# Layer norm, dilated local attention and a gated MLP on one core: half the turns of x move from TensorE to DMA and VectorE, attention's exponentials and loads move back in ScalarE's order

## The chip, the core and the metric

The kernel runs on one core of a Trainium2 chip. The core has five engines with queues of their own: TensorE (matmuls; PE, and PEld for its weight loads), VectorE (DVE), ScalarE (ACT), GpSimd (POOL) and SyncE (SP), and 16 DMA engines. SP and ACT can issue transfers. TensorE writes its results to PSUM; the other data lies in SBUF, 128 partitions wide. The metric is the device time of one execution in microseconds; lower is better.

## The reference

S is 2048, D is 512, F is 1792. There are 32 heads of 16 values; each position looks at 8 keys, 2 apart, ending with itself.

```python
xn = _layernorm(A_x)
q, k, v = split(xn @ wqkv)                        # 32 heads of 16
idx = pos[:, None] - arange(8)[None, :] * 2       # negative: masked
logits = where(mask, einsum("bhsd,bhswd->bhsw", q, kg) * 0.25, -1e9)
o = einsum("bhsw,bhswd->bhsd", softmax(logits), vg)
s = o @ wo
h = relu(xn @ w1 + b1) ** 2
g = silu(h @ w2 + b2)
out = x + s * g
```

All inputs and the output are float32.

## The kernel before

**Products.** Every large product is made in three passes of float32r: each operand is split into a high part (a float32r copy, by ScalarE) and a low part (what is left, by VectorE or GpSimd), and `PASSES` multiplies high by high, high by low and low by high. A group is 12 matmuls of 128 x 128 by 128 x 512 (four parts of the contraction by three passes) into one PSUM tile. PSUM has three sets of buffers: `acc` (four, `psA`), `h` (two, `psH`) and `tp` (two, `psT`).

**First stage: q, k and v.** x is worked in 16 tiles of 128 rows, in pairs. For tile t, `mean` and `spread` (ScalarE, small work on GpSimd) give the moments, `norm` writes `xn`, `trans` turns it by four TensorE transposes into a `tp` tile, ScalarE copies the high part to `xt`, and `lowx` makes the low part on VectorE. `qkv(t, s)` is a group for s = 0, 1, 2 (q, k, v); ScalarE evacuates it to `stg`, and behind the second tile of a pair the pair goes to the scratch tensors `sq`, `sk` and `sv` in DRAM. The loop (line 508) takes two tiles a, a + 1 a pass, six groups, while the next pair is turned and the pair after that is normalised. The high and low parts of x of tiles 4 to 15 go to the scratch tensor `sx` for the MLP.

**Attention** runs on VectorE (products and sums, no matmul) in 8 units of 256 rows. For a unit: q and k are loaded from DRAM, four steps `qk` (a multiplication and a reduction each), `soft_a` (maximum, subtraction, and the exponential on ScalarE), `soft_b` (sum, reciprocal, multiplication), four steps `av` (again a multiplication and a reduction), `store`. The steps `av` of unit u − 1 stand behind `soft_a` of unit u. q, k and v have one buffer each.

**Second stage: MLP and output.** Four chunks of 512 rows. `up(c, f)` for f = 0 to 13 is a group into one of the two `h` buffers; ScalarE applies relu and the square and writes the high part; `lowh(f)` on VectorE reads the same `h` buffer and makes the low part; `down` for f − 2 adds 12 matmuls to four `acc` tiles. `load_o(u)` loads unit u of attention: it stands in step 7 (u = 2c) and step 12 (u = 2c + 1). `trans_o` turns it by VectorE's 32 x 32 transposes (the load has already moved whole blocks to their places), `lowo` makes the low part, `out_product` multiplies by wo, `gate` adds b2 and applies silu, `finish` multiplies, adds x and stores. The output tiles of the second unit of a chunk are finished in the next chunk, those of the last chunk at the end.

**Who sets the order.** TensorE, VectorE, ScalarE and GpSimd keep the order of the program (`Ordered`, line 62, records each instruction). Two clocks are summed while the program is written: `clock["PE"]` by 227 ns for a matmul and 150 for a transpose, `clock["V"]` by elements per partition / 0.96 + 170 ns for an instruction (lines 41 and 51). Attention is a generator: it yields the due time of its next piece, and `pump` (line 300) lets pieces into VectorE's order while `clock["V"]` plus that time is at most `clock["PE"]` plus a margin (3000 ns in the first stage, −500 or 1000 in the second). `not_before` moves VectorE's clock forward where it has to wait. If a unit isn't stored when `load_o` asks for it, the loop there pumps until it is:

```python
while done_units[0] <= u:
    pump(clock["V"] - clock["PE"] + 4000)
```

The transfers on SP have no such order; the framework's scheduler places them.

Of the kernel before, what the change touches and what calls it, by code (L numbers as in the profile page):

```python
# [14 lines left out]
P = 128  # L15
# [23 lines left out]
WARM2 = 3  # L39

MATMUL, TRANSPOSE, DVE_FIXED, SLACK, LATE, ROOM = 227, 150, 170, 500, 3000, 1000


@with_exitstack
def body(ctx: ExitStack, tc: tile.TileContext, x, wqkv, wo, w1, b1, w2, b2, out):
# [121 lines left out]
    mask = const.tile([P, BI, W], F32, name="mask")  # L167
    zero = px.tile([HALO, 4, P], F32, name="zero")

    def constants():  # L170
        G.memset(zero, 0.0)
# [10 lines left out]
    b2t = const.tile([P, D], F32, name="b2t")  # L182

# [7 lines left out]

    done_tiles = dict(qk=0, v=0)
    done_units = [0]

    def load_u(what, u):
        n = BI if what == "q" else WIN
        src = dict(q=sq, k=sk, v=sv)[what]

        t = att.tile([P, n, P], F32, name=f"{what}{u}", tag="k" if (what, u) == ("v", NU - 1) else what)
        row = src[0, u * UP:u * UP + 1, :]  # L200
        ap = bass.AP(tensor=row.tensor, offset=row.offset, ap=[[BI * P, NB], [src.shape[1] * P, 4], [1, n * P]])
        dma(t.rearrange("p i c -> p (i c)"), ap)
        return t

    def attention():

        tiles, Ls, sums = {}, {}, {}
# [13 lines left out]

        def soft_a(u):
            yield 1500
            L = Ls[u]
            if u == 0:
                lm = L.rearrange("p (i h) w -> p i h w", h=8)
                V.tensor_add(lm, lm, mask[:, :, None, :].to_broadcast([P, BI, 8, W]))
            mx = att.tile([P, BI * 8], F32, name=f"mx{u}", tag="mx")  # L230
            V.tensor_reduce(out=mx, in_=L, axis=AX.X, op=OP.max)
            V.tensor_sub(L, L, mx[:, :, None].to_broadcast([P, BI * 8, W]))
            A.activation(L, L, AF.Exp)

        def soft_b(u):
            yield 2100
            L = Ls[u]
            sm = att.tile([P, BI * 8], F32, name=f"sm{u}", tag="sm")
            V.tensor_reduce(out=sm, in_=L, axis=AX.X, op=OP.add)
            V.reciprocal(sm, sm)  # L240
            V.tensor_mul(L, L, sm[:, :, None].to_broadcast([P, BI * 8, W]))

        def av(u, s):
            i0 = 2 * s
            v, L = tiles["v", u], Ls[u]
            yield 2400
# [18 lines left out]
        def load(u, names):  # L265
            if u < NU:
                while done_tiles[names] < 2 * (u + 1):
                    yield None
                for n in names:
                    tiles[n, u] = load_u(n, u)  # L270

        yield from load(0, "qk")
        not_before(clock["PE"] + 8000)
        yield from load(0, "v")

        for u in range(NU + 1):
            if u < NU:
                Ls[u] = att.tile([P, BI * 8, W], F32, name=f"L{u}", tag="L", bufs=2)
                for s in range(4):
                    yield from qk(u, s)  # L280
                yield from soft_a(u)
                yield from load(u + 1, "qk")
                if u == NU - 1:
                    yield from load(u, "v")
            if u == 0:
                yield from soft_b(0)
            for s in range(4):
                if u > 1 or (u == 0 and s < 2) or (u == 1 and s >= 2):
                    yield from av(max(u - 1, 0), s)
            if u:  # L290
# [38 lines left out]
    NT = S // P  # L329
    mv, means, rs, shifts, xn, pTs, xt, xT, seen = {}, {}, {}, {}, {}, {}, {}, {}, {}  # L330

# [25 lines left out]
    def norm(t):  # L357
        xn[t] = px.tile([P, D], F32, name=f"xn{t}", tag="xn", bufs=2)
        if t < 2:
            n = D // 2 if t == 0 else D  # L360
            for i in range(0, D, n):
                V.tensor_scalar(xn[t][:, i:i + n], xins[t][:, i:i + n], mv[t][:, 0:1], rs[t],
                                op0=OP.subtract, op1=OP.mult)
            del xins[t]
        else:
            A.activation(xn[t], xins.pop(t), AF.Identity, bias=shifts.pop(t), scale=rs[t])
        if t + 4 < NT:
            load_x(t + 4)

    def place(t):  # L370
        if t < TPC:
            xt[t] = xT[0][:, t]
        else:
            xt[t] = pxT.tile([P, 2, KT, P], FR, name=f"xt{t}", tag="xt", bufs=4)

    def trans(t):
        place(t)
        pTs[t] = psT(f"pxT{t}")
        for kt in range(KT):
            PE.transpose(pTs[t][:, kt * P:(kt + 1) * P], xn[t][:, kt * P:(kt + 1) * P], ident)  # L380
        seen[t] = clock["PE"] + 800
        A.activation(xt[t][:, 0], pTs[t].rearrange("p (k n) -> p k n", k=KT), AF.Copy)
# [7 lines left out]
    def qkv(t, s, between=None):  # L390
        if t % 2 == 0:
            stgs[s] = pstg.tile([P, 4, 2, P], F32, name=f"stg{t}_{s}", tag="stg", bufs=4)
        ps = psA(f"pq{t}_{s}")
        n = 0
        for kt in range(KT):
# [3 lines left out]
            if between and kt == 1:  # L399
                between()  # L400
        A.activation(stgs[s][:, :, t % 2], ps.rearrange("p (g c) -> p g c", g=4), AF.Copy,
                     scale=0.25 if s == 0 else 1.0)
        if t % 2:
            r0 = (t - 1) * P + (0 if s == 0 else HALO)
            dst = (sq, sk, sv)[s][:, r0:r0 + UP, :].rearrange("g (p e) c -> p g (e c)", e=2)
            dma(dst, stgs[s].rearrange("p g e c -> p g (e c)"))
            done_tiles["qk" if s < 2 else "v"] = t + (s > 0)

# [27 lines left out]


    sts = [px.tile([P, 6], F32, name=f"st{t}", tag="st", bufs=2) for t in range(2)]
    V.bn_stats(sts[0], xins[0])
    moments(0, sts[0])  # L440
    high(*wq_parts(0, 0))
    norm(0)
    low(*wq_parts(0, 0), G)
    V.bn_stats(sts[1], xins[1])
    moments(1, sts[1])
    xT[0] = xTa.tile([P, TPC, 2, KT, P], FR, name="xT0", tag="xT")
    place(0)
    pT = [psT(f"pxT0_{kt}") for kt in (0, 2)]
    for kt in range(KT):
        PE.transpose(pT[kt // 2][:, kt * P:(kt + 1) * P], xn[0][:, kt * P:(kt + 1) * P], ident)  # L450
    for n in range(WARM2):
        PE.transpose(warm[:, :P], ident, ident)
    for kt in (0, 2):
        hi, lo = (xt[0][:, h, kt:kt + 2] for h in range(2))
        src = pT[kt // 2][:, kt * P:(kt + 2) * P].rearrange("p (k n) -> p k n", k=2)
        A.activation(hi, src, AF.Copy)
        V.tensor_sub(lo, src, hi.bitcast(F32))
        if kt == 0:
            high(*wq_parts(0, 1))
    low(*wq_parts(0, 1), V)  # L460
    norm(1)
    split(*wq_parts(0, 2), G)
    split(*wq_parts(0, 3), V)
    clock.update(PE=8000.0, V=10000.0)

    def highs(s, kt):
# [6 lines left out]

    def first():
        trans(1)
        highs(1, 0)
        mean(2)

    qkv(0, 0, first)
    lowx(1)  # L480
    lows(1, 0)
    spread(2)
    qkv(1, 0, lambda: highs(1, 2))
    lows(1, 2)
# [23 lines left out]
    for a in range(2, NT, 2):  # L508
# [11 lines left out]
        qkv(a, 0)  # L520
        if more:
            trans(a + 2)
        pump(LATE)
        qkv(b, 0)
        weights(a - 5)
        if more:
            lowx(a + 2)
            trans(b + 2)
        if later:
            mean(b + 4)  # L530
        pump(LATE)
        qkv(a, 1)
        if later:
            spread(a + 4)
        if more:
            lowx(b + 2)
        pump(LATE)
        if not more:
            up(0, 0)
        qkv(b, 1)  # L540
        if later:
            spread(b + 4)
        if not more:
# [5 lines left out]
        qkv(a, 2)  # L549
        if later:  # L550
            norm(a + 4)
        pump(LATE)
        qkv(b, 2)
        if later:
            norm(b + 4)
        if a == NT - 4:
            dma(b1t, b1.rearrange("(f p) -> p f", p=P))
            dma(b2t, b2[None, :].to_broadcast([P, D]))
        if a >= TPC:
# [69 lines left out]

    wot = p2.tile([P, 2, 4, 512], FR, name="wot")  # L630

    for c in range(NCH):
# [113 lines left out]
```

## Time and profile before

| | us |
|---|---|
| median of 3 runs | 505.66 (503.79 to 506.11) |
| the profiled execution | 507.61 |
| its span | 505.8 |
| matmul on TensorE, busy | 495.2 |
| VectorE, busy | 418.4 |
| ScalarE, busy | 214.2 |
| granted TensorE clock, share of full | 0.998 |

The profile is of one execution. Its rows have the start in us, the duration, the engine, the line, the operation, output <- input, shape and count; in brackets stands the idle time before it and what ended it. Merged rows (x12, x48) cover several instructions. A matmul's duration holds its way through the array, so rows overlap; the distance from start to start is its cost. Most line numbers are that of the recording helper (L74), so rows are told apart by the tiles: `pq` is a group of `qkv`, `pxT` a transpose of x, `ph` is `up`, `pb` is `down`, `pw` is `out_product`, `pr` and `L` are the steps `qk`, `pv` and `v` the steps `av`, `h` on DVE is `lowh`. In this trace, the matmul that is first of the MLP starts at 144.0 us.

### The profile page before, as it was taken

The numbers are of one execution on the slowest core, as the hardware profiler recorded it, in microseconds if no ns is written. First come the engines' busy times: TensorE is split into PE (matmuls) and PEld (weight loads), VectorE is DVE, ScalarE is ACT, GpSimd is POOL, SyncE is SP. The second block draws the span as 40 slices with busy tenths as digits, with TensorE's granted clock in tenths as the row PEclk, the third lists the DMA queues.
The fourth block names the chain that finished last, engine by engine and source line by source line (L and its number), as shares of the span: only waits on it lengthen the run. The fifth ranks groups of instructions, "written<-read, shape, count | busy, mean of one in ns | idle before, by whom it ended". The sixth has DMA issues, their size and how long they took to land.

```text
span 505.8 us, 5934 instructions
## 1 busy us (share of the span) xinstructions
PE 495.2 (98%) x2209; PEld 406.4 (80%) x2209; DVE 418.4 (83%) x327; ACT 214.2 (42%) x393; POOL 119.5 (24%) x127
## 2 busy tenths in 40 slices
PE   7999989999999999999999999999999999999996
PEld 5788878878787888888888888888888878888885
DVE  5208999999999999997799999589998859995244
ACT  4955275573333556431722442263224136223321
POOL 3622076484000399700203000020200002120000
PEclk9999999999999999999999999999999999999999
DMA  8888787689947774643323515344241612112022
GB/s 293 248 260 296 250 322 230 237 312 338 323 141 238 210 227 141 193 165 158 114 65 144 198 41 183 140 123 158 75 173 33 238 44 84 62 64 83 0 84 84
DMA packets 45064, 85.64 MB, mean 169 GB/s; under 512 B 4988, under 2 KB 28908, under 8 KB 42220
## 3 DMA queue, kind: packets, MB, share of 16 engines
q1 hardware_dynamic: 44172, 78.98, 47.2%
q10 hardware_dynamic: 864, 6.29, 3.4%
q8 instruction: 17, 0.28, 0.2%
q14 instruction: 11, 0.09, 0.1%
HBM read 57.94 MB, written 27.32 MB: 169 GB/s over the span
## 4 chain that ended last, share of the span: by engine, by line
PE 70%; DVE 17%; issue 4%; ACT 3%; DMA 3%; POOL 3%; POOLq 0%; ACTq 0%; DVEq 0%
PE pb L74 30%; PE ph L74 29%; PE pw L74 9%; DVE L L74 5%; DVE pr L74 5%; DMA x<-in_A_x 3%; PE pq L74 3%; DVE v L74 2%; DVE pv L74 2%; ACT scratch L74 1%; POOL rs L74 1%; POOL wq L74 1%; DVE xt L74 1%; ACT stg L74 1%; DVE xn L74 1%
## 5 line engine op out<-in xcount | busy, mean ns | idle before, releaser
L74 PE MATMUL pb<-w,h 128*128 128x512 f32 x672 | 160.6, 389 | 0.0
L74 PEld LDWEIGHTS pb<-w,h 128*128 128x128 f32 x672 | 126.1, 188 | 26.2
L74 PE MATMUL ph<-xU,w 128*128 128x512 f32 x504 | 120.7, 390 | 0.0
L74 ACT ACTIVATE ph<-ph,b1t 128x512 f32<-128x512 f32 x56 | 37.0, 661 | 193.0 <-PE ph L74 187.3
L74 PEld LDWEIGHTS ph<-xU,w 128*128 128x128 f32 x504 | 94.3, 188 | 20.6 <-DVE h L74 0.9
L74 PE MATMUL pq<-wq,xt 128*128 128x512 f32 x432 | 101.6, 392 | 0.9 <-ACT stg L74 0.9
L74 PEld LDWEIGHTS pq<-wq,xt 128*128 128x128 f32 x432 | 80.3, 188 | 17.8 <-ACT stg L74 1.4
L74 DVE TENSOR_TENSOR pr<-k,q 128x2048 f32<-128x2048 f32 x32 | 77.0, 2407 | 14.0 <-DMA x<-in_A_x 13.6
L74 DVE TENSOR_TENSOR pv<-v,L 128x2048 f32<-128x2048 f32 x32 | 75.6, 2362 | 0.5
L74 DVE TENSOR_TENSOR h<-ph,h 128x512 fp32r<-128x512 f32 x56 | 38.4, 685 | 42.8 <-ACT ph L74 42.8
L74 DVE TENSOR_REDUCE L<-pr 128x128 f32<-128x2048 f32 x32 | 73.0, 2282 | 0.7
L74 DVE TENSOR_REDUCE v<-pv 128x256 f32<-128x2048 f32 x32 | 72.9, 2280 | 0.6
L74 POOL TENSOR_TENSOR z<-z,xr 128x512 f32<-128x512 f32 x12 | 21.2, 1778 | 219.3 <-DVE z L74 212.5
L74 PE MATMUL pw<-wot,oT 128*128 128x512 f32 (+1 forms) x204 | 45.5, 376 | 0.0
L74 ACT ACTIVATE stg<-pq 128x512 f32<-128x512 f32 x48 | 28.3, 595 | 35.6 <-PE pq L74 35.6
L74 PEld LDWEIGHTS pw<-wot,oT 128*128 128x128 f32 x204 | 36.8, 188 | 7.1
L74 PE MATMUL ph<-xT,w 128*128 128x512 f32 x168 | 40.6, 391 | 0.1
L74 PEld LDWEIGHTS ph<-xT,w 128*128 128x128 f32 x168 | 31.5, 188 | 7.1 <-DVE h L74 0.5
L74 PE MATMUL pq<-wq,xT 128*128 128x512 f32 x144 | 36.2, 402 | 0.6 <-DVE wq L74 0.4
L74 POOL TENSOR_TENSOR w<-w1r,w 128x512 fp32r<-128x512 f32 x14 | 22.1, 1580 | 60.9 <-DMA rwo<-in_A_wo 49.6
L74 POOL TENSOR_TENSOR w<-w2r,w 128x512 fp32r<-128x512 f32 x14 | 34.5, 2466 | 0.0
L74 ACT ACTIVATE h<-ph 128x512 fp32r<-128x512 f32 x56 | 33.7, 601 | 1.8
(54 smaller groups left out, 325.7 us busy)
## 6 DMA issues: line engine op xcount, KB each, us to landing
k<-sk SPq DMA_DIRECT2D x8, 1408.0 KB, 8.2
v<-sv SPq DMA_DIRECT2D x8, 1408.0 KB, 7.9
sx<-xt SPq DMA_DIRECT2D x12, 512.0 KB, 4.8
xU<-sx ACTq DMA_DIRECT2D x6, 1024.0 KB, 5.7
x<-in_A_x SPq DMA_DIRECT2D x16, 256.0 KB, 6.0
sq<-stg SPq DMA_DIRECT2D x8, 512.0 KB, 5.2
q<-sq SPq DMA_DIRECT2D x8, 512.0 KB, 4.2
sk<-stg SPq DMA_DIRECT2D x8, 512.0 KB, 4.9
```

The lines of the kernel that those rows point to most:

```text
L74: return tc.keep_in_program_order(f(*a, **k))
```

## The change

- **x of tiles 6 to 15** (`TURN = 6`). `norm` writes the pair's `xn` in blocks of 32 columns; `shuffle` moves, by 16 transfers from SBUF to SBUF, block a of rows 32b to 32b + 31 to partitions 32a to 32a + 31 of a tile `xb` that shares two buffers with `xn`; `trans` turns 32 x 32 blocks by one VectorE instruction into the same `tp` tile as before. In the loop, `spread`, `norm`, `trans` and `lowx` of these tiles move: `norm` from behind groups 5 and 6 to behind groups 2 and 3, `trans` one group later, `lowx` likewise.
- **Exponentials.** `soft_a` no longer issues the exponential; `defer` keeps it until `clock["PE"]` has passed `clock["V"]` + 5000 ns, and the next `pump` emits it. `soft_b` waits for that. Unit 0's softmax is done in two halves.
- **Loads of q, k and v** are issued by ScalarE's queue instead of SP, and are deferred likewise; their landing is foreseen 9500 ns after they are emitted, and `qk` and `av` are not placed earlier.
- **First q product.** Tile 0's product with the q weights takes four float32 matmuls from unsplit x and weights (`x0`, `raws`); three transposes that filled time (`WARM2`) and the GpSimd part of these splits go.
- **Places.** `zero` shares the buffer of q; `b2t` is loaded at the start of the second stage.

```diff
+TURN = 6
+BEHIND, LAND, LOAD = 5000, 6000, 9500
...
-        dma(t.rearrange("p i c -> p (i c)"), ap)
+        A.dma_start(t.rearrange("p i c -> p (i c)"), ap)
...
+    behind = []
+
+    def defer(t, f):
+        behind.append((t, f))
+        behind.sort(key=lambda b: b[0])
+
+    def flush(t):
+        while behind and (t is None or behind[0][0] <= t):
+            behind.pop(0)[1]()
...
         def qk(u, s):
             i0 = 2 * s
+            yield from there("k", u)
...
+        def there(n, u):
+            while (n, u) not in tiles:
+                yield None
+            not_before(landing[n, u])
...
-            A.activation(L, L, AF.Exp)
+            def exp():
+                A.activation(L, L, AF.Exp)
+                exps.add((u, h))
+
+            defer(clock["V"] + BEHIND, exp)
...
+        def soft_b(u, h=None):
+            while (u, h) not in exps:
+                yield None
...
+            def start():
                 for n in names:
                     tiles[n, u] = load_u(n, u)
+                    landing[n, u] = clock["PE"] + LOAD
+
+            defer(max(clock["V"] + BEHIND if u else 0, done_tiles[names][1][u] + LAND), start)
...
-        not_before(clock["PE"] + 8000)
...
         limit = clock["PE"] + margin
+        flush(clock["PE"])
...
+            A.activation(xn[t // 2 * 2][:, :, t % 2].rearrange("p a (k c) -> p k a c", k=KT),
+                         xins.pop(t).rearrange("p (k a c) -> p k a c", a=4, k=KT),
+                         AF.Identity, bias=shifts.pop(t), scale=rs[t])
...
+    def shuffle(t):
+
+        src = xn.pop(t)
+        xb[t] = px.tile([P, 4, 2, P], F32, name=f"xb{t}", tag="xn", bufs=2)
+        for b in range(4):
+            for a in range(4):
+                dma(xb[t][32 * a:32 * a + 32, b], src[32 * b:32 * b + 32, a])
...
+            V.transpose(out=pTs[t].rearrange("p (k b n) -> p b k n", k=KT, n=32),
+                        in_=xb[t // 2 * 2][:, :, t % 2].rearrange("p b (k c) -> p b k c", k=KT))
+            seen[t] = clock["V"] + 800
...
+    ps = psA("pq0_0")
+    for kt in range(KT):
+        if kt == KT - 1:
+            trans(1)
+        PE.matmul(ps, x0[:, kt * P:(kt + 1) * P], raws[0, kt], start=kt == 0, stop=kt == KT - 1)
     lowx(1)
+    evacuate(0, 0, ps)
+    highs(1, 0)
     lows(1, 0)
+    mean(2)
+    clock.update(PE=12000.0, V=12500.0)
...
     def load_o(u):
         while done_units[0] <= u:
+            flush(None)
             pump(clock["V"] - clock["PE"] + 4000)
```

More of the change, by code (lines that the diff above doesn't have):

```diff
@@ L435, in lowh @@
         V.tensor_sub(h[:, 1], ph, h[:, 0].bitcast(F32))
[L438 to L464, printed above, removed]
     def highs(s, kt):
@@ L472, in lows @@
         low(*wq_parts(s, kt + 1), G)
[L474 to L479, printed above, removed]
+    sts = [px.tile([P, 6], F32, name=f"st{t}", tag="st", bufs=2) for t in range(2)]
+    V.bn_stats(sts[0], xins[0])
+    moments(0, sts[0])
+    high(*wq_parts(0, 0))
+    norm(0)
+    xT[0] = xTa.tile([P, TPC, 2, KT, P], FR, name="xT0", tag="xT")
+    place(0)
+    pT = [psT(f"pxT0_{kt}") for kt in (0, 2)]
+    for kt in range(KT):
+        PE.transpose(pT[kt // 2][:, kt * P:(kt + 1) * P], xn[0][:, kt * P:(kt + 1) * P], ident)
+    V.bn_stats(sts[1], xins[1])
+    moments(1, sts[1])
+    low(*wq_parts(0, 0), V)
+    x0 = scratch(0)
+    for kt in (0, 2):
+        cols = slice(kt * P, (kt + 2) * P)
+        A.activation(x0[:, cols], pT[kt // 2][:, cols], AF.Copy)
+    norm(1)
+    for kt in range(1, KT):
+        split(*wq_parts(0, kt), V)
+    split(xt[0][:, 0], xt[0][:, 1], x0.rearrange("p (k n) -> p k n", k=KT), V)
+    ps = psA("pq0_0")
+    for kt in range(KT):
+        if kt == KT - 1:
+            trans(1)
+        PE.matmul(ps, x0[:, kt * P:(kt + 1) * P], raws[0, kt], start=kt == 0, stop=kt == KT - 1)
     lowx(1)
+    evacuate(0, 0, ps)
+    highs(1, 0)
     lows(1, 0)
+    mean(2)
+    clock.update(PE=12000.0, V=12500.0)
+    qkv(1, 0, lambda: highs(1, 2))
     spread(2)
-    qkv(1, 0, lambda: highs(1, 2))
     lows(1, 2)
@@ L520, in body @@
         qkv(a, 0)
-        if more:
+        if a + 2 < TURN:
             trans(a + 2)
+        if later:
+            spread(a + 4)
+            mean(b + 4)
         pump(LATE)
@@ L525, in body @@
         weights(a - 5)
-        if more:
+        if a + 2 < TURN:
+            lowx(a + 2)
+            trans(b + 2)
+        elif more:
+            trans(a + 2)
+        if later:
+            norm(a + 4)
+            spread(b + 4)
+        pump(LATE)
+        qkv(a, 1)
+        if a + 2 < TURN:
+            lowx(b + 2)
+        elif more:
             lowx(a + 2)
@@ L529, in body @@
         if later:
[L530 to L536, printed above, removed]
+            norm(b + 4)
+            shuffle(a + 4)
         pump(LATE)
@@ L630, in body @@
     wot = p2.tile([P, 2, 4, 512], FR, name="wot")
+    b2t = p2.tile([P, D], F32, name="b2t")
+    dma(b2t, b2[None, :].to_broadcast([P, D]))
     for c in range(NCH):
```

83 lines of the change are left out of this document (49 added, 34 removed).

## The prediction

> **What bounds the kernel now.** I read the page first, then TensorE in order of time, then what the other engines were late with, then VectorE's end against TensorE's steps in the last two chunks.
>
> ```profile
> span 505.8 us, 5934 instructions
> PE 495.2 (98%) x2209; PEld 406.4 (80%) x2209; DVE 418.4 (83%) x327; ACT 214.2 (42%) x393; POOL 119.5 (24%) x127
> DVE  5208999999999999997799999589998859995244
> ```
>
> TensorE is busy for 98% of the span, so time can only come from matmul work taken off it or from its few gaps. VectorE (the slices) is full from about 40 us to the middle of the run and has holes later: it is the engine whose place in order matters.
>
> ```profile
> 46.20 2.91 PE L74 MATMUL pq<-wq,xt 128*128 128x512 f32 x12
> 48.95 0.60 PE L74 MATMUL pxT<-ident,xn 128*128 128x128 f32 x4
> 49.31 3.02 PE L74 MATMUL pq<-wq,xt 128*128 128x512 f32 x12
> ...
> 67.84 0.66 PE L74 MATMUL pxT<-ident,xn 128*128 128x128 f32 x4 [1.45 <-ACT xn L74]
> ...
> 102.75 0.66 PE L74 MATMUL pxT<-ident,xn 128*128 128x128 f32 x4 [0.18 <-ACT xn L74]
> ...
> 132.98 11.18 PE L74 MATMUL pq<-wq,xt 128*128 128x512 f32 x48 [0.95 <-ACT stg L74]
> 144.00 2.94 PE L74 MATMUL ph<-xT,w 128*128 128x512 f32 x12
> ```
>
> The first row is the start of `qkv(4,0)`, the last that of `up(0,0)`: 97.80 us for 33 groups of 12 matmuls. A group is 2.72 us (the rows of the chain below), 33 are 89.76. So **8.0 us** of this stage are no group: the transposes of tiles 6 to 15 (48.95 to 49.31, 0.36 us for a tile, and a little at the next group) and three gaps behind ScalarE. What held ScalarE:
>
> ```profile
> 61.89 0.63 ACT L74 ACTIVATE L<-L 128x512 f32<-128x512 f32 x1 [7.83 <-DVE L L74]
> 97.46 0.63 ACT L74 ACTIVATE L<-L 128x512 f32<-128x512 f32 x1 [6.18 <-DVE L L74]
> 131.81 0.63 ACT L74 ACTIVATE L<-L 128x512 f32<-128x512 f32 x1 [10.47 <-DVE L L74]
> ```
>
> Each exponential stood in ScalarE's queue 6 to 10 us before VectorE had its logits; each gap follows one of these.
>
> Now the other end. The chain of waits gives TensorE's steps, the timeline VectorE's:
>
> ```profile
> 387.20 2.72 PE ph L74 x12
> 447.31 2.72 PE ph L74 x12
> 474.50 2.72 PE ph L74 x12
> 496.26 5.60 PE pw L74 x36
> ```
>
> ```profile
> 39.71 2.29 DVE L74 TENSOR_TENSOR pr<-k,q 128x2048 f32<-128x2048 f32 x1 [13.62 <-DMA x<-in_A_x]
> 49.95 2.29 DVE L74 TENSOR_TENSOR pr<-k,q 128x2048 f32<-128x2048 f32 x1
> 52.27 2.29 DVE L74 TENSOR_REDUCE L<-pr 128x128 f32<-128x2048 f32 x1
> 368.27 2.29 DVE L74 TENSOR_REDUCE v<-pv 128x256 f32<-128x2048 f32 x1
> 433.04 2.29 DVE L74 TENSOR_REDUCE v<-pv 128x256 f32<-128x2048 f32 x1
> 457.92 2.28 DVE L74 TENSOR_REDUCE v<-pv 128x256 f32<-128x2048 f32 x1
> 485.12 1.31 DVE L74 STREAM_TRANSPOSE pT<-oq 128x512 f32<-128x512 f32 x2
> 490.25 0.69 DVE L74 TENSOR_TENSOR z<-pb,b2t 128x512 f32<-128x512 f32 x1 [0.79 <-PE pb L74]
> 495.69 1.36 DVE L74 TENSOR_TENSOR z<-pb,b2t 128x512 f32<-128x512 f32 x2
> 502.35 0.42 DVE L74 TENSOR_TENSOR z<-z,xlast 128x256 f32<-128x256 f32 x1
> ```
>
> The three `ph` rows are `up(2,12)`, `up(3,7)` and `up(3,12)`: behind them the program asks for units 5, 6 and 7 of attention (`load_o`). They end at 389.9, 450.0 and 477.2; the units' last reductions ended at 370.6, 435.3 and 460.2. Slack now: 19.4, 14.7 and 17.0 us. An attention piece costs 2.32 us (49.95 to 52.27).
>
> **The change part by part.** *Transposes and the exponentials: −8.0, of which I take −7.5.* All 8.0 us go if ScalarE is never late. Instead VectorE gets ten transposes, and SP sixteen small transfers for each of five pairs:
>
> ```profile
> L74 DVE STREAM_TRANSPOSE pT<-oq 128x512 f32<-128x512 f32 x16 | 10.5, 701 | 0.0
> oq<-so SPq DMA_DIRECT2D x32, 128.0 KB, 3.4
> 464.70 1.73 SPq L587 DMA_DIRECT2D oq<-so  x4
> k<-sk SPq DMA_DIRECT2D x8, 1408.0 KB, 8.2
> ```
>
> ```profile
> 94.42 0.52 SPq L202 DMA_DIRECT2D k<-sk  x1
> 15.15 3.55 SPq L558 DMA_DIRECT2D b2t<-in_B_b  x1
> ```
>
> By the pair above, 0.65 us of VectorE for each tile. Nearest row for a transfer from 32 partitions to 32 is `oq`: 0.43 us of issue, 3.4 us to landing. Sixteen take 6.9 us of SP and 3.4 more, from the third group of one pass of the loop to the second of the next, five groups or 13.6 us: covered. At `k`'s 8.2 us the transposes come some 3 us late; ScalarE waits in front of them, and the four `acc` buffers let TensorE run three groups (8.2 us) ahead. Cover gone costs the part over 8.2 us. Bounds −8.9 (0.9 for a gain I don't see) to −5. The q, k and v loads leave SP (24 issues of 0.52 us) for ScalarE's queue, behind times that the planner foresees; a load that finds its store not landed holds the evacuations behind it, under the same 8.2 us.
>
> *Head: 0.*
>
> ```profile
> 11.37 6.80 PE L74 MATMUL pq<-wq,xT 128*128 128x512 f32 x28
> 16.98 1.30 POOL L74 TENSOR_TENSOR wq<-wqraw,wq 128x512 fp32r<-128x512 f32 x1
> 18.33 0.73 PE L74 MATMUL pq<-wq,xT 128*128 128x512 f32 x2 [0.17 <-POOL wq L74]
> ```
>
> Four float32 matmuls replace twelve of 0.227 us (2.72). No row has one: between 0.9 us (a rate of 0.227) and 3.6 (each as four). Either way TensorE meets GpSimd's low part of the k weights, which ended at 18.28 and keeps its place in GpSimd's order, so an earlier start is waited away there. −1 to +0.9; I take 0. By the Trainium skill, "FP8 and Floating Point Precision", TensorE Precision Notes, true float32 is four passes, which is the upper bound; the sum would be the same.
>
> *The order of VectorE: +19.3.* This is where the change decides. `pump` (line 300) places attention by two sums of prices: a piece is emitted while VectorE's clock plus its due time stays under TensorE's clock plus a margin. I added both up along the program by the prices of line 41. For the kernel before, unit 6 is stored at V 430.2 and asked for at PE 444.7, unit 7 at 455.1 and 471.9, unit 5 at 366.4 and 384.7: slack 14.5, 16.8 and 18.3, as in the rows above. These clocks say what stands in front of what, not how long it takes.
>
> The change moves both. The first piece may stand at V 36.3 (load emitted at PE 26.8, plus `LOAD` 9.5) where it stood at 29.4: +6.9, though on the chip it began at 39.71 only, and its k load moves by under a microsecond. Ten transposes at 703 ns: +7.0. Unit 0's softmax in halves, six more fixed parts of 170 ns: +1.0. Waiting for unit 1's landing: +1.3. TensorE's clock loses 40 × 150 ns and starts 0.7 later: −5.3. Together 21.5 us against slacks of 14.5, 16.8 and 18.3: short by 7.0, 4.7 and 3.2. That is the least. A step of 5.45 us has room for two pieces and a `lowh` (2 × 2.30 + 0.70), and a piece that misses is lost to the step, so the full sum is worse: when `load_o(5)` comes, 6 pieces are missing, for units 6 and 7 seven each. Then the loop in `load_o` emits them all at once, ahead of `lowh`.
>
> ```profile
> L74 DVE TENSOR_TENSOR h<-ph,h 128x512 fp32r<-128x512 f32 x56 | 38.4, 685 | 42.8 <-ACT ph L74 42.8
> 460.23 0.57 SPq L262 DMA_DIRECT2D so<-v  x1
> ```
>
> Unit 5: from 1.8 us before `up(2,12)` ends, 6 × 2.32 and `lowh(12)` 0.6 end 12.7 us behind it; its product `down` comes five groups behind, 13.6. Hidden, 0.
>
> Unit 6: VectorE is free 1.4 us before `up(3,7)` ends (previous pieces, `lowh(6)` and one `finish`). 7 × 2.32 = 16.3 and 0.6: `lowh(7)` ends 15.5 us behind. There are two `ph` buffers, and `up(9)` takes that of `up(7)` 8.16 us behind it (three groups). **TensorE stalls 7.3 us** (4.9 to 9.6 with a piece less or more). It will be idle long enough to come back slow:
>
> ```profile
> 1.35 4.10 PE L74 MATMUL warm<-ident 128*128 128x128 f32 x18 [1.35 <-POOL mhalf L74]
> ```
>
> The 18 first transposes took 0.23 us each, against 0.09 in the stage above (0.36 for four): 2.5 us lost in a start from rest. I take half, +1.2 (0 to 2.5). The Trainium skill, "TensorE: Matmul & The Clock Gate", Why this matters for your kernels, says that no gap should be over about 3 us, or the clock falls to half; by the page's window of 3.4 us that is an estimated 1.7 us, and the sum would be 518.0. The trace's granted clock shows no such fall.
>
> Unit 7: VectorE is free 2.2 us before `up(3,12)` ends, and the last reduction ends 14.1 behind. From 460.2 the store, four `oq` loads and their landing took to about 469.5 (460.23, 464.70 with 1.73, then 3.4): 9.3 us. So the last transposes start 23.4 behind, where they stood 7.9 behind (485.12). The low parts end at 26.3, the gates and first two finishes take 6.8 (490.25 to 497.05), the last two 3.3: end 36.4 behind. It was 25.6 (502.77 less 477.2). **+10.8** (8.5 to 13.1 with a piece less or more). Matmuls run out earlier, at about 30.6, so stalls of TensorE in between cost nothing more.
>
> Other moves: the `b2t` load (3.55 us of SP) goes to the start of the second stage, a whole chunk ahead of the first `gate`; `zero` only changes its place. 0.
>
> **Sum**, against the profiled execution's 507.6 (span 505.8): −7.5 + 0 + 7.3 + 1.2 + 10.8 = +11.8, or 519.4. That execution lies 1.9 above the median of the runs, 505.66; from that I forecast **517.5**.
>
> **The rivals.** *The backlog does no harm: faster.* VectorE's real place decides: with three pieces left at unit 6 `lowh(7)` ends before 8.16, with two at unit 7 the end stays. The least shortage above (3 and 2 pieces) is just that. For it: VectorE waits for `h` 42.8 us in all, so it has time. Against: these waits lie behind a `lowh` in a fixed order, and the pieces stand behind them. 505.66 − 7.5 = 498.2.
>
> *Half of it.* Four pieces each: stall 0.3, end (4 − 2) × 2.32 = 4.6: 503.1.
>
> *x comes late.* The transfers meet the stage's other traffic:
>
> ```profile
> GB/s 293 248 260 296 250 322 230 237 312 338 323 141 238 210 227 141 193 165 158 114 65 144 198 41 183 140 123 158 75 173 33 238 44 84 62 64 83 0 84 84
> ```
>
> Slices 9 to 11 (101 to 139 us) move 312 to 338 GB/s, near the most of the run, and each pass adds half a megabyte. If landing doubles from 8.2 to 16.4, transposes are 11.7 late, 3.5 over the cover, for three pairs: +10.5, on top of the forecast 528.0. Against: `oq` landed in 3.4.
>
> **How the numbers follow.** Forecast 0.68, half 0.10, no harm 0.15, x late 0.07. The forecast's own range, with its terms' bounds and not all at one end, is 510 to 524. For 8 in 10 I add the half case and a little more below: 502 to 525. A measurement of this kernel tells about 0.5% (2.5 us) from no change. Faster 0.15 + 0.03, same 0.04, slower 0.68 + 0.07 + 0.03.
>
> **What would show it.** The stage from `qkv(4,0)` to `up(0,0)` should have no 128x128 rows after tile 5 and last about 90.3 us. ScalarE's waits for `L` should be near 0. In chunk 3 VectorE should show seven `pv`/`v` rows without a break, then `h`, and TensorE a gap of about 7 us in front of a `ph` group; `STREAM_TRANSPOSE` of unit 7 should start about 23 us behind `up(3,12)`. Wrong if `h` rows stand between those pieces, if the last `v` reduction ends before `up(3,12)`, or if gaps in the first stage grow.

## The result, and the profile after

The changed kernel takes 537.42 us (median of 4 runs, 535.36 to 537.92) against 505.88 for the kernel before on the same chip: a ratio of 1.0639, 95% interval 1.0612 to 1.0667. It is slower, as forecast, but by 31.5 us and not by 11.8, and far above the forecast's range of 510 to 524. The profiled execution took 537.67 with a span of 535.6; its page begins so:

```profile
span 535.6 us, 5954 instructions
PE 499.5 (93%) x2162; PEld 406.3 (76%) x2162; DVE 423.0 (79%) x344; ACT 218.6 (41%) x397; POOL 99.5 (19%) x125
```

TensorE's share fell from 98% to 93%, and no other engine took its place: everybody waits more. Cut at TensorE's own marks, the span of before and of after divides like this (us; each mark is the start or end of a group in TensorE's timeline):

| stretch | before | after | difference | forecast |
|---|---|---|---|---|
| up to `qkv(4,0)` | 46.20 | 45.95 | −0.2 | 0 |
| first stage, `qkv(4,0)` to `up(0,0)` | 97.80 | 107.92 | **+10.1** | −7.5 |
| `up(0,0)` to the end of `up(3,7)` | 305.9 | 306.8 | +0.9 | 0 |
| to the end of `up(3,12)` | 27.2 | 38.3 | +11.1 | +8.5 |
| to VectorE's last instruction | 25.7 | 33.9 | +8.2 | +10.8 |

The last two rows, the order of VectorE, make 19.3 together, as forecast. The whole miss is in the first stage: 17.6 us. TensorE's rows after idle time, in order of time (start, duration, in brackets the gap and what ended it):

```profile
102.28 18.84 PE L78 MATMUL pq<-wq,xt 128*128 128x512 f32 x72 [7.10 <-ACT stg L78]
124.62 17.94 PE L78 MATMUL pq<-wq,xt 128*128 128x512 f32 x72 [3.49 <-ACT stg L78]
143.96 0.73 PE L78 MATMUL pq<-wq,xt 128*128 128x512 f32 x2 [1.40 <-ACT stg L78]
...
174.35 3.06 PE L78 MATMUL ph<-xT,w 128*128 128x512 f32 x12 [1.02 <-DVE h L78]
...
477.37 5.38 PE L78 MATMUL ph<-xU,w 128*128 128x512 f32 x12 [8.40 <-DVE h L78]
513.57 8.77 PE L78 MATMUL pb<-w,h 128*128 128x512 f32 x31 [2.47 <-DVE h L78]
```

Three gaps behind ScalarE, again, but larger than those of before, and without an exponential in front. ScalarE's waits in the first stage (what waited for what: us in total, times, longest):

```profile
ACT xt L78 <- DVE pxT L78: 36.4, 7, 11.4
ACT xt L78 <- DMA sx<-xt: 10.4, 2, 7.8
ACT stg L78 <- PE pq L78: 8.9, 7, 2.2
```

The exponentials' waits (24 us in three) are gone; in their place ScalarE stands in front of the copy of a turned tile, which VectorE hasn't turned, or whose `xt` buffer is still waiting to be stored. VectorE in turn waits for x (its transposes with a gap over 1 us in front):

```profile
57.18 0.73 DVE L78 STREAM_TRANSPOSE pxT<-xb 128x512 f32<-128x512 f32 x1 [5.24 <-DMA xb<-xn]
...
98.99 0.73 DVE L78 STREAM_TRANSPOSE pxT<-xb 128x512 f32<-128x512 f32 x1 [5.46 <-DMA xb<-xn]
...
142.06 0.73 DVE L78 STREAM_TRANSPOSE pxT<-xb 128x512 f32<-128x512 f32 x1 [7.11 <-DMA xb<-xn]
```

And SP, to which these waits lead (its timeline: start, duration from the first issue to the last, and the count), with the transfers' row on the page (KB each, us from issue to landing):

```profile
63.10 10.02 SPq L440 DMA_DIRECT2D xb<-xn  x16
73.22 0.53 SPq L481 DMA_DIRECT2D sk<-stg  x1
73.85 0.45 SPq L481 DMA_DIRECT2D sv<-stg  x1
...
80.88 16.58 SPq L440 DMA_DIRECT2D xb<-xn  x16
97.56 0.53 SPq L481 DMA_DIRECT2D sk<-stg  x1
...
126.15 14.24 SPq L440 DMA_DIRECT2D xb<-xn  x16
```

```profile
xb<-xn SPq DMA_DIRECT2D x80, 32.0 KB, 1.9
```

A transfer lands in 1.9 us, faster than I took. But sixteen of them hold SP for 10.02 us when nothing delays them (0.63 us each), and for up to 16.6; the stores of k, v and q stand behind the block. What SP waits for inside such a block, longest first (first stage, same columns as ScalarE's waits):

```profile
SPq L440 <- DMA sx<-xt: 4.7, 2, 2.4
SPq L440 <- ACT stg L78: 3.7, 2, 2.5
SPq L440 <- DMA xb<-xn: 3.2, 4, 2.2
SPq L440 <- DMA x<-in_A_x: 2.6, 2, 2.3
...
SPq L440 <- DMA sq<-stg: 2.1, 1, 2.1
SPq L440 <- DMA w2r<-in_B_w: 1.9, 1, 1.9
```

SP's issue waits mostly for *other* transfers to land. The semaphores named in the trace's records of these transfers say why: the transfers on SP and on ScalarE's queue raise eight semaphores as completion counters, SP's block takes them in turn, and 74 of the 80 `xb` transfers wait for the very counter that they raise next, that is for the landing of the transfer that used it last. So a block of sixteen goes twice round the eight, and its first half waits for the stores and loads issued before it: in the block at 80.88 these are the fourth, fifth and seventh transfer, issued at 84.75, 87.71 and 91.26 only.

The order part can be read from VectorE's timeline at unit 6: one piece after another without `h` between them (seven from 460.50 to 476.63), then two `h` at once.

```profile
459.30 0.68 DVE L78 TENSOR_TENSOR h<-ph,h 128x512 fp32r<-128x512 f32 x1
...
460.50 2.28 DVE L78 TENSOR_REDUCE v<-pv 128x256 f32<-128x2048 f32 x1
...
474.43 2.29 DVE L78 TENSOR_REDUCE v<-pv 128x256 f32<-128x2048 f32 x1
476.63 1.28 DVE L78 TENSOR_TENSOR h<-ph,h 128x512 fp32r<-128x512 f32 x2
...
520.39 1.32 DVE L78 STREAM_TRANSPOSE pT<-oq 128x512 f32<-128x512 f32 x2 [6.28 <-DMA oq<-so]
```

### The profile page after: what moved, and what is told of

The parts are those of the page before. It is cut to its first block, busy times and chain, and to the rows that moved or that the text cites. A ratio compares the mean times of both kernels' runs of the same rounds, so it can differ in the third digit from the quotient of the medians.

```text
span 535.6 us, 5954 instructions
## 1 busy us (share of the span) xinstructions
PE 499.5 (93%) x2162; PEld 406.3 (76%) x2162; DVE 423.0 (79%) x344; ACT 218.6 (41%) x397; POOL 99.5 (19%) x125
## 4 chain that ended last, share of the span: by engine, by line
PE 50%; DVE 20%; DMA 10%; SPq 7%; issue 5%; ACT 5%; POOL 2%; ACTq 0%; DVEq 0%; POOLq 0%
PE ph L78 22%; PE pb L78 21%; PE pw L78 6%; SPq L440 6%; DMA x<-in_A_x 4%; DVE L L78 4%; DVE pr L78 3%; DVE pv L78 3%; DVE v L78 3%; DMA xb<-xn 3%; ACT scratch L78 1%; DMA sx<-xt 1%; POOL rs L78 1%; DVE h L78 1%; ACT xn L78 1%
## 5 line engine op out<-in xcount | busy, mean ns | idle before, releaser
L78 PE MATMUL pb<-w,h 128*128 128x512 f32 x672 | 162.4, 392 | 2.5 <-DVE h L78 2.5
L78 PE MATMUL ph<-xU,w 128*128 128x512 f32 x504 | 123.1, 396 | 8.4 <-DVE h L78 8.4
L78 PEld LDWEIGHTS ph<-xU,w 128*128 128x128 f32 x504 | 95.9, 191 | 29.7 <-DVE h L78 9.7
L78 PE MATMUL pq<-wq,xt 128*128 128x512 f32 x432 | 103.8, 401 | 12.9 <-ACT stg L78 12.0
L78 PEld LDWEIGHTS pq<-wq,xt 128*128 128x128 f32 x432 | 83.2, 194 | 33.0 <-ACT stg L78 13.7
L78 DVE TENSOR_TENSOR pr<-k,q 128x2048 f32<-128x2048 f32 x32 | 75.2, 2349 | 10.1 <-DMA k<-sk 9.7
L78 POOL TENSOR_TENSOR z<-z,xr 128x512 f32<-128x512 f32 x12 | 19.3, 1616 | 221.1 <-DVE z L78 163.3
L78 POOL TENSOR_TENSOR w<-w1r,w 128x512 fp32r<-128x512 f32 x14 | 27.1, 1936 | 67.7 <-DMA w2r<-in_B_w 52.9
L78 PE MATMUL pq<-wq,xT 128*128 128x512 f32 x132 | 32.9, 402 | 1.8 <-POOL wq L78 1.5
L78 ACT ACTIVATE ph<-ph 128x512 f32<-128x512 f32 x56 | 33.3, 595 | 0.0
```

What stands on the lines that cost most here:

```text
L78: return tc.keep_in_program_order(f(*a, **k))
```

## The experiments

My theory after this reading was that the sixteen transfers hold SP, and the order of VectorE makes the end late, two separate losses. The rivals: x itself comes too late; the bytes crowd the DMA engines; the late end follows from the late first stage. "First stage" is the stretch from `qkv(4,0)` to `up(0,0)` in each trace. All kernels start from the changed one. A time of theirs without a ratio beside it is that of a single run.

**The order alone (523.68 us).** Attention gets more lead in the second stage.

```diff
-MATMUL, TRANSPOSE, DVE_FIXED, SLACK, LATE, ROOM = 227, 150, 170, 500, 3000, 1000
+MATMUL, TRANSPOSE, DVE_FIXED, SLACK, LATE, ROOM = 227, 150, 170, -2000, 3000, 2000
```

> The changed kernel with the planner's second-stage margins raised from -500 and 1000 ns to 2000 and 2000, so that by the planner's sums no unit of attention is missing when it is asked for. Theory (two independent costs: x late in the first stage, and the order of VectorE in the last chunk): the 8.6 us gap in front of up(3,9), the slow group behind it and the late end go, about 19 us, and the first stage stays at 108 us; span about 516. Rival (VectorE has too much to do, whatever its order): the waits only move, span over 528.

The late end went (VectorE's last instruction ends at 518.8, 23.0 us behind the start of `up(3,13)`, as in the profile before, 479.78 to 502.77), while the first stage kept its 106.4 us: two losses, and the late end isn't a consequence of the first. But the time missed 516, since the lead brought new stalls early on:

```profile
167.60 3.02 PE L78 MATMUL ph<-xT,w 128*128 128x512 f32 x12 [1.31 <-DVE h L78]
175.04 3.02 PE L78 MATMUL ph<-xT,w 128*128 128x512 f32 x12 [1.71 <-DVE h L78]
210.67 3.01 PE L78 MATMUL ph<-xT,w 128*128 128x512 f32 x12 [2.27 <-DVE h L78]
255.97 3.04 PE L78 MATMUL ph<-xU,w 128*128 128x512 f32 x12 [1.48 <-DVE h L78]
```

**No turns by VectorE (504.61, then a median of 504.48 over 12 runs).** `TURN = 16`: everything of the change but the transfers and VectorE's transposes.

> The changed kernel with TURN = 16: all of x is turned by TensorE again, no transfers from SBUF to SBUF; deferred exponentials, loads on ScalarE's queue and the float32 product stay. Theory (the sixteen issues a pair on SP make x late): the stage from qkv(4,0) to up(0,0) falls from 107.9 us to about 95 (97.8 before, less the 3 us of gaps behind the exponentials); by the planner's sums two pieces are missing at units 5, 6 and 7, which hides; span about 502 to 504. Rival (loads and late exponentials hold ScalarE): the stage stays over 104, span over 512.

> The changed kernel with all transposes on TensorE, once more and in rounds. The one look gave 504.61 against 505.89. Theory: the rest of the change (exponentials and loads further back on ScalarE) is worth 3 us in the first stage and gives 1 to 2 back at the end: ratio 0.995 to 0.999. Rival: no difference from before, ratio 0.999 to 1.002.

The first stage was 94.5 us (45.87 to 140.34), against 97.80 before, with no gap, and no unit was late at the end. The ratio is 0.9984, interval 0.9969 to 1.0: a gain of about 1 us that the runs hardly tell from none. Between the two profiles the first stage is 3.3 us shorter with the exponentials and loads in their new places, and nothing of that is lost later: from `up(0,0)` to the end both take 361.8 us. The medians differ by less because the profiled execution of before (507.61) lies 1.7 us above the median of the runs beside it (505.87). Which stretch of it was longer than usual can't be said from one trace, so part of the 3.3 may belong to that execution.

**The transfers without a reader (519.34).** All transposes on TensorE, and beside them sixteen transfers a pair into a tile that nothing reads.

```diff
+        src = xn[t + 1]
+        spare = px.tile([P, 4, 2, P], F32, name=f"spare{t}", tag="spare")
         for b in range(4):
             for a in range(4):
-                dma(xb[t][32 * a:32 * a + 32, b], src[32 * b:32 * b + 32, a])
+                dma(spare[32 * a:32 * a + 32, b].rearrange("p e c -> p (e c)"), src[32 * b:32 * b + 32, 256 * (a % 2):256 * (a % 2) + 256])
```

> All transposes on TensorE, and at the place of the transfers sixteen transfers of the same shape and size a pair into a spare tile that nobody reads. Theory A (SP's queue is the cost: q, k and v stores, sx stores and x loads stand behind the sixteen): the first stage grows from 94.6 us to 97 to 103, with ScalarE waits for x or for xt's buffers, none for pxT. Theory B (the cost is only that VectorE, and ScalarE behind it, wait for the moved x): the stage stays at 94.5 to 96.

The first stage went from 94.5 to 109.3, more than theory A asked for. ScalarE's waits there:

```profile
ACT xt L78 <- DMA sx<-xt: 13.8, 1, 13.8
ACT stg L78 <- DMA sk<-stg: 10.1, 1, 10.1
ACT w L78 <- DMA w2r<-in_B_w: 9.9, 1, 9.9
ACT stg L78 <- DMA sx<-xt: 7.9, 1, 7.9
ACT xn L78 <- DMA spare<-xn: 3.8, 1, 3.8
```

Nobody needs the moved data, and yet 14.9 us are lost: what is late are the stores and loads of others that stand behind the block, and the buffers (`xt`, `stg`, the weights) that they free or fill. The last row is a tie that is left: the unread transfers still read `xn`, and once ScalarE waits 3.8 us for that buffer. What this row alone costs was not tried.

**Half as many (504.54).** `for b in range(2)` in the same kernel: eight unread transfers a pair.

> All transposes on TensorE and eight unread transfers a pair instead of sixteen. With sixteen the first stage grew by 14.9 us (94.4 to 109.3). If the loss is by the number of transfers, the stage is about 102 (half); if it is what goes beyond the slack of the stores, under 98.

94.5 us: nothing is lost. The price isn't per transfer: eight hide in SP's slack (blocks of 5 to 6.3 us), sixteen do not.

**VectorE's turns without the transfers (517.93, median of 4).**

```diff
-        src = xn.pop(t)
-        xb[t] = px.tile([P, 4, 2, P], F32, name=f"xb{t}", tag="xn", bufs=2)
-        for b in range(4):
-            for a in range(4):
-                dma(xb[t][32 * a:32 * a + 32, b], src[32 * b:32 * b + 32, a])
+        xb[t] = xn.pop(t)
```

> The changed kernel without the sixteen transfers: VectorE turns the 32x32 blocks of x where they lie, so the blocks of different partitions are not exchanged (the output is not the reference's). VectorE's order, its ten transposes and everything else stay. If the transfers alone were the missed term and the rest of the prediction holds: first stage 90 to 91.5 us, the seven-piece runs and the late end as in the changed kernel, 516 to 520 us. If VectorE's own lateness also costs the first stage: 94 to 98 us there, 521 to 526. If the late end comes from the delay of the first stage and not from the order: under 510.

Ratio 1.0245, interval 1.0214 to 1.0276. TensorE's first group of the MLP, and its rows after idle time in the whole run behind 46 us:

```profile
135.77 2.94 PE L78 MATMUL ph<-xT,w 128*128 128x512 f32 x12
...
457.95 5.17 PE L78 MATMUL ph<-xU,w 128*128 128x512 f32 x12 [8.41 <-DVE h L78]
493.95 7.32 PE L78 MATMUL pb<-w,h 128*128 128x512 f32 x31 [2.47 <-DVE h L78]
503.16 7.48 PE L78 MATMUL pw<-wot,oT 128*128 128x512 f32 x36 [1.90 <-DVE oT L78]
```

From 45.97 to 135.77 are 89.8 us without a gap, the 33 groups and nothing else; then the forecast's stall and late end. Without the transfers the kernel takes what I forecast for the change (517.5). With them it takes 19.5 us more, 18.1 of these in the first stage. That stage's groups of TensorE in the changed kernel and in this one (busy, mean ns of a matmul, idle before):

```profile
L78 PE MATMUL pq<-wq,xt 128*128 128x512 f32 x396 | 95.2, 402 | 12.9 <-ACT stg L78 12.0 <-DVE xt L78 0.9
```

```profile
L78 PE MATMUL pq<-wq,xt 128*128 128x512 f32 x396 | 90.0, 389 | 0.0
```

12.9 us of gaps and 5.2 of slower matmuls: the 18.1. This kernel also spares the buffer of `xb`, which the changed one shares with `xn`; there the transfers waited 1.1 us for VectorE to free it, so that is not the loss.

**Five larger transfers instead of sixteen (523.78).** One store of 512 KB to DRAM and four loads of 128 KB that bring the blocks to their places.

```diff
+        xd = dram.tile([4, P, 2 * P], F32, name=f"xd{t}")
+        dma(xd.rearrange("a r n -> r a n"), src.rearrange("p a e c -> p a (e c)"))
+        for a in range(4):
+            dma(xb[t][32 * a:32 * a + 32].rearrange("p b e c -> p b (e c)"),
+                xd[a].rearrange("(b p) n -> p b n", p=32))
```

> The changed kernel with each pair's sixteen transfers replaced by five: one store of xn to DRAM and four loads of 128 KB, as load_o has them. More bytes, fewer issues. Theory (SP's issue time, about 0.63 us each, and its waits between issues): ScalarE's waits for VectorE's transposes fall from 36 us to under 10, the stage from 107.9 to 91 to 96, span 519 to 523, with the end as late as in the changed kernel. Rival (the DMA engines are full, bytes decide): the stage stays over 105.

96.0 us, with twice the bytes: the traffic isn't the cause. ScalarE still waited 36.6 us for turned tiles, not under 10. My reading was that the rest is x that comes late, two trips instead of one; a later experiment tests it. The sum of these waits doesn't measure the loss: it is 36.4 us in the changed kernel, which loses 18.1, 36.6 here, where 6.2 are lost, and 18.1 without the transfers, where nothing is.

**On GpSimd's queue (534.33).**

```diff
-                dma(xb[t][32 * a:32 * a + 32, b], src[32 * b:32 * b + 32, a])
+                G.dma_start(xb[t][32 * a:32 * a + 32, b], src[32 * b:32 * b + 32, a])
```

> The changed kernel with the sixteen transfers a pair issued by GpSimd's queue instead of SP's. Theory: SP's time, its issues and the waits that they stand behind, makes the loss of the first stage; the landing itself takes about 2 us. If GpSimd's issue takes no longer than SP's 0.63 us, the stage falls from 107.9 to 92 to 98 us, ScalarE's waits for pxT to under 20 us, and the whole to 520 to 526. If GpSimd takes over 1 us an issue, its own work (the small steps of the next norm, the splitting of weights) is late and the stage stays over 105. Rival (small transfers as such are slow or crowd the DMA engines, whoever issues them): stage 105 to 109.

The stage stayed at 104.8, which by its number can't be told from the rival's 105. The waits speak for the block, which moved and kept its kind: GpSimd issued in 0.50 us each, but waited 16.7 us in 13 places for its own transfers, which now took 4.4 us to land, and its small steps of the next norm (ScalarE waited 25.3 us for `mean`) and the splitting of weights came late. The trace's records give GpSimd's transfers eight counters of their own, and eight issues take 4.0 us, less than the 4.4 to landing, which fits the waits. That small transfers as such are slow is answered by the eight unread ones, which cost nothing. By the Trainium skill, "Perfetto Trace Analysis", DMA Optimizations, balancing transfers over the engines that can issue them may help when the generation of descriptors is the bottleneck; here all sixteen went to another engine, and that brought 3.1 of 18.1 us, since that queue had work of its own behind the block.

**Four parts of four (544.74), and the same with more lead from the second chunk on (525.72, median of 4, ratio 1.0386, 1.0356 to 1.0415).**

```diff
         qkv(b, 1)
...
+        if later:
+            shuffle(a + 4, 1)
...
         qkv(a, 2)
+        if later:
+            shuffle(a + 4, 2)
...
         qkv(b, 2)
+        if later:
+            shuffle(a + 4, 3)
```

`shuffle(t, b)` issues the four transfers of one b. In the second kernel `ROOM` is 3000 and `pump`'s own margin too for c over 0 (`lead[0] = 3000 if c else -SLACK`).

> The changed kernel with the sixteen transfers of a pair put into SP's order in four parts of four, one behind each of four groups, instead of in one block. Theory A1 (the block is the cost: q, k, v and sx stores and x loads stand behind 10 to 17 us of SP at once): the first stage falls from 107.9 us to 92 to 97 and the whole to 522 to 526, since the late end of the order stays. Theory A2 (the number of transfers is the cost, since each takes 0.63 us of SP and a landed one of eight counters): the stage stays over 103.

> The transfers in four parts of four, and attention with more lead from the second chunk on (margins +3000 and +3000 ns; the first chunk keeps -500), where by the two sums of prices no unit is short by more than a piece. If both losses go as parts: first stage 92 to 97 us, no forced run of seven pieces, end within 27 us of up(3,12): 498 to 505 us. If late lowh steps stall TensorE in chunk 1 as they did with +2000 everywhere: 505 to 511. If the first stage does not fall: over 511.

A1 fails: the stage grew to 117.3. That is over A2's 103, but not for A2's reason: the number of transfers is the same, and the stage grew by 9.3 us. SP's order is the scheduler's, which put parts together again (rows of x8 and x12), and the sixteenth transfer of a pair was issued later than in the changed kernel, at 56.9 against 55.1 for the first pair and 146.8 against 139.8 for the last, while the transposes kept their places: ScalarE waited 57.5 us for them. The block was bad for what stood behind it; spread out, it was bad for its reader. The second kernel does show the order's remedy: from `up(0,0)` at 162.9 to the end 361.1 us, as before the change (144.0 to 505.8), without one stall.

**Five transfers and lead together (513.79, median of 4, ratio 1.0174, 1.014 to 1.0208).** The lead is that of the first experiment.

> Both: five transfers a pair and the raised margins. Theory (the two costs are independent and add up): span 497 to 503, faster than before by 0.5 to 1.5%. Rival (one cost hides behind the other): over 508.

Missed: the first stage's 96.2 and the four early stalls (6.75 us) stayed. Alone the order saved 13.7 us of 537.42 and the five transfers 13.6, together 23.6, 3.7 less than the sum of two single runs: they nearly add up, but neither was whole.

**Five transfers with the loads three groups behind the store, and each transpose one group later (529.44); then with more lead (508.01, median of 12, ratio 1.0046, 1.0028 to 1.0064).**

```diff
-        elif more:
-            trans(a + 2)
...
         elif more:
-            lowx(a + 2)
-            trans(b + 2)
+            trans(a + 2)
...
         if TURN <= a + 2 < NT:
-            lowx(b + 2)
+            lowx(a + 2)
+            trans(b + 2)
...
         qkv(a, 2)
+        if TURN <= a + 2 < NT:
+            lowx(b + 2)
         pump(LATE)
         qkv(b, 2)
+        if later:
+            fetch(a + 4)
```

`shuffle` now holds the store to DRAM alone and `fetch` the four loads.

> Five transfers a pair through DRAM as before (one of 512 KB out, four of 128 KB back), but with the four back put three groups behind the one out, and each transpose one group later in the order. If the 6 us that the first stage still lost with five transfers (96 us against 89.8 without any) come from x that lands behind the transposes' place, the stage falls to 90 to 93 and the whole to 517 to 521, with ScalarE's waits for pxT under 20 us. If they come from the bytes or from SP's turn among more transfers, the stage stays at 95 to 98 and the whole over 522.

> The same, with attention's margins at +3000 ns from the second chunk on. With those margins (and the first chunk's left at -500) the second stage and the end took 361 us, as before the change, with no stall. First stage 90 to 93: 498 to 502 us, faster than before by 0.8 to 1.5% and faster than all transposes on TensorE (503.7). With a stage of 95 to 98: 503 to 506.

The first stage fell to 92.7, as x's lateness would have it (ScalarE's waits for turned tiles to 20.4, a little over the 20 asked for), but both whole times missed. In the first kernel the second stage's stalls grew (9.14, 4.21 and 2.17 us); that the later transposes push attention back in the order is the likely reason, and was not tried by itself. In the second the first stage took 93.6, and units 6 and 7 were still short: `h` came late by 1.12 us at 457, and the end stood 25.9 us behind the start of `up(3,13)` instead of 23.0.

**Both taken away.** With all transposes on TensorE (`TURN = 16`, `SLACK` −500, `ROOM` 1500): 503.68 us, median of 12, ratio 0.9973, 0.9957 to 0.999.

> The changed kernel with all transposes on TensorE (no transfers of x) and with VectorE's order given more lead in the second stage (margins +500 and +1500 ns instead of -500 and +1000). If the first stage's loss is the transfers' and the end's loss the order's, both are gone: first stage about 95 us, no forced run of attention pieces, 500 to 505 us. If more lead brings stalls on late lowh in the early chunks, as it did with margins of +2000, 506 to 511.

And the five late transfers with `SLACK` −500 (a margin of +500) in the first chunk and +3000 in the others: **502.30 us, median of 7, ratio 0.9942, 0.9919 to 0.9965**, the lowest of all. The two intervals overlap, so it is not shown that this kernel beats the one with all transposes on TensorE; both are faster than before, by under 1%.

> As e14_late_order, with the first chunk's margin at +500 ns instead of -500. By the two sums of prices units 6 and 7 were still three pieces short in e14 (and its trace showed one late h of 1.12 us and an end some 4 us late); with +500 none is short. If the sums hold: first stage 92.5 to 95 us, then 361 to 362.5, no stall over 0.5 us: 500.5 to 504. If the chunk-0 margin stalls TensorE on late lowh steps as +2000 did: 505 to 509. Rival that wins nothing: over 506 with no stall.

Its TensorE rows after idle time behind 46 us are three, all in the first stage (93.4 us), and the rest takes 361.6, as expected:

```profile
96.61 3.75 PE L78 MATMUL pq<-wq,xt 128*128 128x512 f32 x14 [1.50 <-ACT xt L78]
100.72 29.76 PE L78 MATMUL pq<-wq,xt 128*128 128x512 f32 x130 [0.36 <-DVE xt L78]
130.73 8.75 PE L78 MATMUL pq<-wq,xt 128*128 128x512 f32 x36 [0.26 <-ACT xt L78]
```

## Why the prediction was right or wrong, point by point

- **Transposes and exponentials, −7.5: wrong, and alone to blame.** The 8.0 us were there to be had: 97.80 less 89.8 without the transfers, 3.3 from the exponentials' and loads' places and 4.7 from the transposes (up to 1.9 of the 8.0 may belong to the one profiled execution of before, which is that much over its median). The failed step is "sixteen take 6.9 us of SP and 3.4 more ... five groups or 13.6 us: covered", with its bounds of −8.9 to −5. It took 0.43 us an issue from the `oq` row, where the block takes 0.63 each and 10.0 to 16.6 us with its waits. Worse, it asked only whether x would come in time. What stands *behind* the sixteen on SP was not asked: the unread transfers lose 14.9 us with nobody waiting for what they move. The 3 us between that and 18.1 may be the readers' share; that was not tried by itself. The prediction's own sign of being wrong, that gaps in the first stage grow, is what came.
- **The loads on ScalarE's queue holding the evacuations: not seen.** ScalarE's waits name the copies of turned tiles and the stores, and with all transposes on TensorE the loads stay there and the stage has no gap.
- **Head, 0: right** (−0.2). A float32 matmul (two records each) cost about four times the 0.227 us of the others: the first three took 2.7 us (6.63 to 9.31), the fourth 0.85 (9.75 to the next group at 10.60).

```profile
6.63 2.84 PE L78 MATMUL pq<-wqraw,scratch 128*128 128x512 f32 x6
9.31 0.60 PE L78 MATMUL pxT<-ident,xn 128*128 128x128 f32 x4
9.75 1.02 PE L78 MATMUL pq<-wqraw,scratch 128*128 128x512 f32 x2
```

- **Order of VectorE, +19.3: right in kind, and in sum by luck.** Seven pieces at unit 6 and seven at unit 7 stand without a break, as counted from the two sums of prices. The stall was 8.4 us where 7.3 was forecast (4.9 to 9.6), the slow restart 2.5 where I took 1.2, the late end 8.2 where I had 10.8, just under its bounds. That the sum is right to the tenth is luck: 2.6 too little in the stretch to `up(3,12)` and 2.6 too much behind it. Behind `up(3,12)` the last reduction ended 14.0 us later, as forecast (14.1), but from there (512.92) to the last transposes (520.39) it took 7.5 us instead of 9.3.
- **The clock.** I took half of what the head's row showed, because no row of before showed a fall; there was no such gap to show it. The profile after has it (windows after three gaps: us, PE busy with count, granted clock, DMA share, GB/s):

```profile
102.28:104.28 2.00, 2.00 (x5) 0.50 0.95 209
104.28:106.28 2.00, 2.00 (x6) 0.50 1.13 362
...
124.60:126.60 2.00, 1.98 (x5) 0.50 0.87 346
...
477.40:479.40 2.00, 2.00 (x5) 0.50 0.65 262
479.40:481.40 2.00, 2.00 (x7) 0.50 0.29 90
```

  Half speed behind a gap, as the rule of the Trainium skill that the prediction cites has it; it lasted 3 to 5 us by such windows, so a gap cost up to 2.5 us on top, not 1.7. Most of the first stage's 5.2 us of slower matmuls is this. The rule's limit of about 3 us is not borne out: behind the gap of 2.47 us at 513.57 the clock was 0.50 too (7 matmuls from 513.57 to 516.57). Without the transfers the same gap, at 493.95, left it at 1.00 (13 matmuls in 3 us), and behind one of 1.90 at 503.16 it was 0.50 from 503.57 to 506.97. The measurement decides: a gap's length alone didn't tell whether the clock fell.
- **The rivals.** "Backlog harmless" and "half of it" are out: all seven pieces were in place. "x comes late" (528.0) had the right stage and the wrong mechanism: transfers landed in 1.9 us, not 16.4; SP was late with them and with all the others. Its sum was also wrong: sixteen issues of 6.9 us and a landing of 8.2 are 1.5 us over the cover of 13.6, not some 3, and with 16.4 they are 9.7 over it, not 11.7, so 1.5 over the 8.2 and not 3.5.
- **Small.** The stall of 1.02 at 174.35 was not foreseen: it is gone without the transfers and with five instead of sixteen (stage of 96.0 us), so the first stage's delay is the likely reason.

## What to carry to other kernels

When transfers are added to a queue, first list what will stand behind them there and which buffer each of those frees; count the transfers as well as their bytes, at the price of an issue from a row of the same form, and look whether an issue waits for earlier landings. A queue has a slack: here the cost was nothing within it and steep beyond it (eight: 0, sixteen: 14.9 us). Where an order is made by sums of prices, walk the sums again after any change: here they gave the number of late pieces at units 6 and 7 exactly. Moving a margin is the cheap remedy, but not without a price: 2000 ns in all chunks made four early stalls of 6.75 us together, and 500 in the first chunk with 3000 from the second on made none.

## What was not expected of the hardware

- A transfer of 32 KB from SBUF to SBUF cost SP 0.63 us from issue to issue (10.02 us for sixteen), more than one of 128 KB from DRAM in the profile before (0.43).
- Gaps of 3.49 to 8.40 us in front of TensorE were followed by half the granted clock for 3 to 5 us in the profile after; the gaps of 1.31 to 2.27 us in the first experiment left a group at its usual time (3.02 us for 12). In between it went both ways: 2.47 us was followed by 0.50 in the profile after and by 1.00 without the transfers, where 1.90 us was followed by 0.50.
- The share of the loss that is SP's issue time and the share that is its waits for the eight counters weren't told apart.
